# Block-causal attention and a maxout feed-forward in one kernel: group 2's q and k requested behind group 1's, its scores and exps among the units of M, group 3's q and k beside w1

## The chip, the cores and the metric

The kernel runs on one core of one Trainium2 chip. The metric is the device time of one execution in microseconds (us). Before the change it is 260.99 us, the median of four runs (259.36 to 264.78).

## What is computed

Eight batches, eight heads, 576 positions of 64 numbers each; the mask is causal by blocks of 64. The attention output, as 4,608 tokens of 512 numbers, goes through a feed-forward layer with two parallel weights and a maximum between them.

```python
scores = scale * np.matmul(q, k.transpose(0, 1, 3, 2))
mask = block_i >= block_j                      # blocks of 64
scores = np.where(mask, scores, -1000000000.0)
attn = np.exp(scores - np.max(scores, axis=-1, keepdims=True))
attn = attn / (np.sum(attn, axis=-1, keepdims=True) + 1e-09)
x = np.matmul(attn, v)                         # then to (B * S, H * D)
h1 = x @ w1
h2 = x @ w2
out = np.maximum(h1, h2) @ w_out
```

## The kernel before, in words

**Groups and pairs.** Two heads make a pair, two pairs a group: pairs 0 and 1 are group 0, pairs 4 and 5 are group 2. A batch has two groups, so groups 0 and 1 (pairs 0 to 3) are batch 0, and group 2 is the first of batch 1. There are 16 groups.

**What happens to a group.** `load_qk` requests q and k of a group (0.59 MB each) by two DMAs on a queue, SP's as a rule. With `gated=True` GpSimd first writes one element of the buffer, and the DMA waits for that write: so the request goes out when GpSimd's own program has come to this place. `cast` makes bf16 of them (on VectorE and ScalarE for group 0, on VectorE for group 1, on GpSimd from group 2 on). `transposes` turns 18 small blocks of q, or of k, on TensorE into two PSUM tiles, which VectorE and ScalarE copy out to `qT` and `kT`. `pad_keys` (GpSimd) makes the padded keys for the blocks in the corner. The scores of a pair go to PSUM in three tiles (`tile_0` to `tile_2`; for batch 0 in four bursts, `burst_p`, `burst_q1` to `burst_q3`), ScalarE takes the exp of each into `aT`, and GpSimd sets the masked corners to zero. `av(p, ts)` multiplies by V (with a column of ones for the sum) and VectorE divides, into `xp`. `x_out` transposes `xp` on TensorE and copies it into `xT`; later groups do this by a DMA transpose.

**The feed-forward part.** max(h1, h2) is written as max(x(w1 - w2), 0) + x w2. So the kernel needs d = w1 - w2 (four pieces, `diff_w`, VectorE), and M = w2 w_out, so that the second part becomes x M. w2 is transposed in four units (`bT_unit`), M is computed in eight units of eight matmuls (`m_unit`; M0 to M3 use the first half of w_out and are copied out by VectorE, M4 to M7 the second half and ScalarE), then come the units h (`h_unit`: four matmuls of 512 columns, and the maximum with zero on VectorE into `g`) and y (`y_unit`: 12 matmuls).

**How the order is set.** The order on every engine is that of the program: it is written out by hand. `fill(n)` puts the next n parts of the feed-forward units into TensorE's stream (a part of M costs 0.5, of w2's transposes 0.25, of h and y 1), in the order bT, M, h, y; a unit of h or y may only come when its tokens are done. `fill_of(g)` shares out what is ready over the groups to come.

**Queues and buffers.** V, w2, w_out and w1 are requested by GpSimd, on one queue, in the order of its program; V, w2 and w_out are cast to bf16 on the way. Scores have two PSUM tiles, everything else on TensorE (transposes, M, h, y, av, x_out) shares four, in turn: the next user of a tile waits for the copy out of the last one. q and k each have three raw buffers, so that group 2's first request needs no earlier buffer to come free; group 3's take those of group 0.

**The lines concerned** (of the kernel before): `load_qk` 107 to 119, `cast` 121 to 127, `load_v` 129, `load_w1` 147, `diff_w` 154, `h_unit` 191, `m_unit` 217, `transposes` 322 to 341 (matmuls 329, copies 337), `scores` 343, `pad_keys` 354, `exp` 371, `mask` 376, `av` 442, `x_out` 482; the hand-written order is lines 556 to 655. Its parts for batch 0 end at line 614; group 2 and M follow down to line 641, group 3 from 642.

Of the kernel before, what the change touches and what calls it, by code (L numbers as in the profile page):

```python
# [14 lines left out]
def kernel(  # L15
# [28 lines left out]
    RPP = S // NP  # L44
# [9 lines left out]
    NCH = 5  # L54
# [52 lines left out]
    def load_qk(g, queues, gated=False):  # L107
        b, u = divmod(g, GPB)
        for nm, src, queue in (("q", q, queues[0]), ("k", k, queues[1])):
            if queue is None:  # L110
                continue
            raws[nm, g] = t = raw.tile([P, 2, RPP * D], FP32, name=f"{nm}raw")
            if gated:
                nc.gpsimd.memset(t[:, 0, :1], 0.0)
            queue.dma_start(
                out=t[:],
                in_=src[b, 4 * u:4 * u + 4].rearrange(
                    "(s h) (p t) d -> (h p) s (t d)", h=2, t=RPP),
            )

    def cast(nm, g, parts):
        t = raws[nm, g].rearrange("p s (t d) -> p t s d", d=D)
        if (nm, g) not in qk_n:
            qk_n[nm, g] = qkn.tile([P, RPP, 2, D], BF16, name=f"{nm}n")
        n = qk_n[nm, g]
        for copy, j0, j1 in parts:
            copy(out=n[:, j0:j1], in_=t[:, j0:j1])  # L127

    def load_v(b, c):
        rows = min(P, S - c * P)  # L130
        nc.gpsimd.dma_start(  # L131
            out=vv_r[b % NV][P - rows:, c, :, :D],
            in_=v[b, :, c * P:c * P + rows, :].rearrange("h p d -> p h d"),
        )
# [12 lines left out]
    def load_w1(j):  # L147
        w1_raw[j] = wraw.tile([P, NDM, WB], FP32, name="w1raw")
        nc.gpsimd.dma_start(out=w1_raw[j][:], in_=w1r[:, :, j * WB:(j + 1) * WB])
# [4 lines left out]
    def diff_w(j):  # L154
        nc.vector.tensor_sub(d_sb[:, :, j * WB:(j + 1) * WB], w1_raw[j][:], w2_sb[j])
# [9 lines left out]
    SP, ACT = nc.sync, nc.scalar  # L165
# [4 lines left out]
    nc.vector.memset(zeros[:], 0.0)  # L170
    nc.scalar.activation(out=warm[:], in_=warm[:], func=AF.Exp)
    load_qk(1, (SP, SP))
    make_identity(nc, ident)
    for r in range(NV):
        nc.vector.memset(vv_r[r][:, :, :, D:D + 1], 1.0)
# [123 lines left out]
    def fill(n):  # L299
        while n > 0:  # L300
            if not current:
                k = next((k for k, t in enumerate(todo) if t[2] <= done_tokens[0]), None)
                if k is None:
                    return max(0, n)
                current.append(todo.pop(k))
            t = current[0]
            next(t[1])
            n -= t[3]
            t[0] -= 1
            if not t[0]:  # L310
                current.pop()
        return 0
# [10 lines left out]
    def transposes(nm, g, copies):  # L323
        n = qk_n.pop((nm, g))
        pts = [ps_m.tile([P, RPP, NP], BF16, name=f"ps_{nm}T", tag="m") for _ in range(2)]
        for j in range(RPP):
            for i in range(2):
                r = slice(i * NP, (i + 1) * NP)
                nc.tensor.transpose(  # L329
                    pts[i][:, j, :], n[r, j].rearrange("p s d -> p (s d)"), ident[r, r],  # L330
                )

        def copy_out(which=(0, 1), part=(0, NP), copy=None):
            p0, p1 = part
            for i in which:
                t = (qT_r if nm == "q" else kT_r)[(2 * g + i) % NT]
                (copy or copies[i])(  # L337
                    out=t[:, p0 * RPP:p1 * RPP].rearrange("q (p j) -> q p j", j=RPP),
                    in_=pts[i][:, :, p0:p1].rearrange("q j p -> q p j"),
                )  # L340
        return copy_out
# [12 lines left out]
    def pad_keys(p):  # L354
        nc.gpsimd.tensor_copy(
            out=kz_r[p % NT].rearrange("p (a c) -> p a c", c=BLK)[:, 0:3:2],
            in_=kT_r[p % NT][:, S - 3 * BLK:].rearrange("p (a c) -> p a c", c=BLK)[:, 0:3:2],
        )
# [39 lines left out]
    def burst_q3(p, warm=0):  # L398
        burst(p, ((3, 384, 192),), 1408, warm)
# [11 lines left out]
    def tile_0(p):  # L411
        u = ps_s.tile([P, 2, 512], FP32, name="ps_s", tag="s")
        scores(p, u, 0, 0, 0, 512)
        return lambda: (exp(p, u, 512, 0), mask(p, 0))

    def tile_1(p):
        u = ps_s.tile([P, 2, 512], FP32, name="ps_s", tag="s")
        scores(p, u, 0, 0, 512, 64)
        scores(p, u, 64, 1, 128, 448)
        return lambda: (exp(p, u, 512, 512), mask(p, 576))  # L420

    def tile_2(p):
        u = ps_s.tile([P, 2, 512], FP32, name="ps_s", tag="s")
        corner_scores(p, u, 320)
        scores(p, u, 0, 2, 256, 320)
        scores(p, u, 384, 3, 448, P)

        def out():
            exp(p, u, 512, 1024)
            nc.scalar.activation(  # L430
                out=aT_r[p % NA][BLK:, :, 1536:AW], in_=u[BLK:, :, 320:320 + BLK],
                func=AF.Exp, scale=scale,
            )
            mask(p, 1024)
            mask(p, 1344)
        return out

    def region(*tiles):
        for out in tiles:
            out()  # L440

    def av(p, ts):
        b, hp = divmod(p, HP)
        vv = vv_r[b % NV]
        a = aT_r[p % NA]
        n = len(ts)
        h0 = hp // 2 * 4 + hp % 2
        if p % 2 == 0 and ts[0] == 0:
            xps[p // 2] = xpool.tile([P, 2, NCH, 2, D], BF16, name="xp")
        xp = xps[p // 2]  # L450
        po = ps_m.tile([P, n, 2, D + 1], FP32, name="ps_o", tag="m")
        n_mm = 2 * sum(t + 1 for t in ts)
        mm = 0
        for gi, t in enumerate(ts):
            for hh in range(2):
                for c in range(t + 1):
                    a0 = a_col(p, c, t)
                    nc.tensor.matmul(  # L458
                        po[:, gi, hh, :], a[:, hh, a0:a0 + P], vv[:, c, h0 + 2 * hh, :],
                        start=(mm == 0), stop=(mm == n_mm - 1),  # L460
                    )
                    mm += 1
        rec = small.tile([P, 3, 2, 1], FP32, name="rec")
        nc.vector.reciprocal(rec[:, :n, :, 0], po[:, :, :, D])  # L464
        nc.vector.tensor_mul(  # L465
            xp[:, :, ts[0]:ts[0] + n, p % 2].rearrange("q s t d -> q t s d"), po[:, :, :, :D],
            rec[:, :n].to_broadcast([P, n, 2, D]),
        )
# [13 lines left out]
    def x_out(g, t0=0, t1=NCH, copies=(dve, dve)):  # L482
        b, u = divmod(g, GPB)
        if x_by_dma(g):
            if u == GPB - 1:
                done_tokens[0] = (b + 1) * S
            return
        xp = xps[g]
        n = t1 - t0
        n_odd = min(t1, NCH - 1) - t0  # L490
        pe = ps_m.tile([P, 2, n, BLK], BF16, name="ps_xe", tag="m")
        po = ps_m.tile([P, 2, n_odd, BLK], BF16, name="ps_xo", tag="m")
        for s in range(2):
            for t in range(t0, t1):
                src = xp[:, s, t].rearrange("p a d -> p (a d)")
                nc.tensor.transpose(pe[:, s, t - t0, :], src[:BLK], ident[:BLK, :BLK])
                if t < NCH - 1:
                    nc.tensor.transpose(po[:, s, t - t0, :], src[BLK:], ident[BLK:, BLK:])
        dst = xT[:, 2 * u:2 * u + 2, b * S + t0 * P:b * S + t1 * P].rearrange(
            "p s (t h w) -> p s t h w", h=2, w=BLK)  # L500
        copies[0](out=dst[:, :, :, 0], in_=pe[:])
        copies[1](out=dst[:, :, :n_odd, 1], in_=po[:])
        if u == GPB - 1:
            done_tokens[0] = min(b * S + t1 * P, (b + 1) * S)
# [86 lines left out]
    burst_p(3, 1)  # L591
    masks_p(2)
    masks_p(3)
    load_qk(2, (SP, SP), gated=True)
    load_w1(0)
    fill(2)
    av(1, [2, 3, 4])
    burst_q1(2)
# [11 lines left out]
    av(3, [0, 1])  # L610
    burst_q2(3)
    av(2, [2, 3, 4])
    burst_q3(3)
    masks_q(3)
    load_w1(3)
    cast("q", 2, ((pool, 0, RPP),))
    load_qk(3, (SP, SP), gated=True)
    cast("k", 2, ((pool, 0, RPP),))
    load_v(1, 0)
    fill(8)  # L620
    av(3, [2, 3, 4])
    x_out(1, 0, NCH, (act, act))
    fill(4)
    transposes("q", 2, (dve, act))()
    fill(4)
    transposes("k", 2, (dve, act))()
    pad_keys(4)
    pad_keys(5)
    load_v(1, 1)
    diff_w(0)  # L630
    fill(4)
    region(tile_0(4), tile_1(4))
    load_v(1, 2)
    load_v(1, 3)
    fill(8)
    region(tile_2(4), tile_0(5))
    load_v(1, 4)
    diff_w(1)
    fill(8)
    region(tile_1(5), tile_2(5))  # L640
    diff_w(2)
    cast("q", 3, ((pool, 0, RPP),))
    cast("k", 3, ((pool, 0, RPP),))
# [89 lines left out]
```

## Time and profile before

| | |
|---|---|
| runs (us) | 259.36, 262.26, 264.78, 259.72 |
| the profiled execution | 259.36, with a span of 257.5 |
| mean granted TensorE clock | 1.00 |
| moved by DMA | 41.28 MB, mean 160 GB/s |

The span is the time between the first and the last instruction that the profile shows. The page cuts it into 40 equal slices of 6.4 us; each digit is the busy share of a slice in tenths, and the last two rows tell how busy the 16 DMA engines were on the mean, and what they moved in GB/s:

```profile
PE   8897899999999999999999999999999999999995
DVE  4986559656684348433843384338442743543300
ACT  2876394687665857585758574857485611000111
POOL 1984495576556344634472447253721100000000
DMA  7999999989999686998798869985977061202122
GB/s 249 211 160 262 335 306 71 356 99 234 190 159 267 131 270 52 233 155 224 116 265 134 255 73 252 149 244 77 92 130 112 6 89 51 74 6 75 43 106 98
```

PE is TensorE's matmul, DVE VectorE, ACT ScalarE, POOL GpSimd. The stages around the change lie in the first seven slices: up to about 24 us the attention of batch 0, with w2's transposes among it; from 24.91 to about 38 us the units of M with the scores and exps of group 2; then units of h, and group 3's transposes at 42.13 and 44.12 us. From about 47 us on the loop over the groups runs, and after 217 us only h and y are left.

DMA requests of this stage, with the start of the issue in us: group 2's q and k 18.50 and 18.91; group 3's 27.03 and 27.51; the four pieces of w1 18.61, 21.57, about 22.3 and 24.25; the halves of w_out 14.42 and 16.63.

### The profile page before, as it was taken

Reading aid. Unit: us, or ns where it says so; the run is one execution under the profiler, and the core shown is the slowest. Engines: PE = TensorE matmul, PEld = TensorE weight load, DVE = VectorE, ACT = ScalarE, POOL = GpSimd, SP = SyncE. Lnnn points to the kernel's source line nnn. Section 1 sums busy time; section 2 is a strip of 40 time slices with the busy share of each in tenths; the row PEclk is TensorE's granted clock in tenths of the full one; section 3 lists DMA queues with packets and bytes.
Section 4 is the critical chain, followed back from the end, with each engine's and each line's share of the span. In section 5 each row is a group of like instructions: output and inputs, shape, how many; then the busy total and the mean of one; then the engine's idle time right before and its main releaser. Section 6 shows DMA issues by size and latency. Waiting matters only on the chain.

```text
span 257.5 us, 7082 instructions
## 1 busy us (share of the span) xinstructions
PE 248.5 (97%) x2948; PEld 135.6 (53%) x2948; DVE 135.3 (53%) x279; ACT 142.6 (55%) x200; POOL 106.9 (42%) x269
## 2 busy tenths in 40 slices
PE   8897899999999999999999999999999999999995
PEld 2465754556555555555555555555555555444444
DVE  4986559656684348433843384338442743543300
ACT  2876394687665857585758574857485611000111
POOL 1984495576556344634472447253721100000000
PEclk9999999999999999999999999999999999999999
DMA  7999999989999686998798869985977061202122
GB/s 249 211 160 262 335 306 71 356 99 234 190 159 267 131 270 52 233 155 224 116 265 134 255 73 252 149 244 77 92 130 112 6 89 51 74 6 75 43 106 98
DMA packets 71264, 41.28 MB, mean 160 GB/s; under 512 B 53569, under 2 KB 58049, under 8 KB 71233
## 3 DMA queue, kind: packets, MB, share of 16 engines
q1 hardware_dynamic: 28544, 31.27, 43.8%
q0 software_dynamic: 42272, 8.92, 38.8%
q10 hardware_dynamic: 416, 0.66, 0.7%
q8 instruction: 23, 0.38, 0.7%
q14 instruction: 9, 0.07, 0.1%
HBM read 34.60 MB, written 9.44 MB: 171 GB/s over the span
## 4 chain that ended last, share of the span: by engine, by line
PE 83%; POOL 6%; DMA 6%; ACT 1%; issue 1%; DVE 1%; ACTq 0%; POOLq 0%
PE ps_y L240 36%; PE ps_h L198 23%; PE ps_o L458 10%; PE ps_s L348 7%; DMA wo_sb<-in_moe_w_out_dram 4%; POOL vv L131 3%; PE ps_qT L329 2%; DMA qraw<-in_q_dram 2%; PE ps_kT L329 2%; PE ps_M L221 2%; POOL xT L152 1%; PE ps_y L255 1%; POOL aT L377 1%; POOL qn L127 1%; ACT aT L372 1%
## 5 line engine op out<-in xcount | busy, mean ns | idle before, releaser
L372 ACT ACTIVATE aT<-ps_s 128x1024 bf16<-128x1024 f32 (+2 forms) x100 | 95.9, 996 | 22.4 <-PE ps_s L348 20.7
L240 PE MATMUL ps_y<-wo_sb,g 128*128 128x512 bf16 x280 | 70.2, 379 | 0.0
L198 PE MATMUL ps_h<-xT,d_sb 128*128 128x512 bf16 x288 | 68.9, 380 | 0.0
L203 DVE TENSOR_SCALAR g<-ps_h 128x512 bf16<-128x512 f32 x72 | 49.5, 689 | 32.9 <-PE ps_h L198 32.0
L377 POOL MEMSET aT<- 64x128 bf16 x128 | 23.3, 202 | 84.5 <-ACT aT L372 83.7
L458 PEld LDWEIGHTS <-aT 128*128 128x128 bf16 x960 | 37.4, 98 | 14.0 <-issue 0.5
L245 ACT COPY y<-ps_y 128x512 f32<-128x512 f32 x31 | 18.2, 586 | 45.4 <-PE ps_y L240 37.0
L464 DVE RECIPROCAL rec<-ps_o 128x4 f32<-128x4 f32 (+1 forms) x64 | 12.0, 187 | 58.6 <-PE ps_o L458 57.7
L198 PEld LDWEIGHTS <-d_sb 128*128 128x128 bf16 x288 | 26.0, 98 | 30.4 <-issue 3.1
L240 PEld LDWEIGHTS <-g 128*128 128x128 bf16 x280 | 25.7, 98 | 29.3 <-issue 1.9
L458 PE MATMUL ps_o<-vv,aT 128*128 128x65 bf16 x960 | 39.7, 194 | 0.0
L240 PE MATMUL ps_y<-m_sb,xT 128*128 128x512 bf16 x140 | 38.2, 380 | 0.0
L131 POOL DMA_DIRECT2D vv<-in_v_dram x40 | 33.7, 848 | 0.9 <-issue 0.5
L348 PE MATMUL ps_s<-qT,kT 64*128 64x128 bf16 (+6 forms) x344 | 31.6, 280 | 1.4 <-ACT kT L337 0.7
L465 DVE TENSOR_TENSOR xp<-ps_o,rec 128x256 bf16<-128x256 f32 (+1 forms) x64 | 31.4, 491 | 2.2
L240 PEld LDWEIGHTS <-xT 128*128 128x128 bf16 x140 | 12.1, 98 | 15.3 <-issue 3.7
L127 POOL CAST qn<-qraw 128x1152 bf16<-128x1152 f32 (+1 forms) x15 | 17.1, 1137 | 6.6 <-DMA qraw<-in_q_dram 6.5
L337 ACT COPY qT<-ps_qT 128x576 bf16<-128x576 bf16 x15 | 9.6, 639 | 17.9 <-PE ps_qT L329 17.9
L348 PEld LDWEIGHTS <-kT 64*128 64x128 bf16 x344 | 12.0, 94 | 12.2 <-issue 7.9
L337 ACT COPY kT<-ps_kT 128x576 bf16<-128x576 bf16 x15 | 9.6, 638 | 14.1 <-PE ps_kT L329 13.3
L127 POOL CAST kn<-kraw 128x1152 bf16<-128x1152 f32 x14 | 16.1, 1152 | 1.5 <-DMA kraw<-in_k_dram 1.1
L337 DVE COPY qT<-ps_qT 128x576 bf16<-128x576 bf16 x17 | 12.7, 750 | 0.9 <-PE ps_qT L329 0.9
(58 smaller groups left out, 149.9 us busy)
## 6 DMA issues: line engine op xcount, KB each, us to landing
qraw<-in_q_dram SPq DMA_DIRECT2D x16, 576.0 KB, 4.2
out_dram<-y SPq DMA_DIRECT2D x35, 256.0 KB, 3.3
kraw<-in_k_dram SPq DMA_DIRECT2D x15, 576.0 KB, 5.7
vv<-in_v_dram POOLq DMA_DIRECT2D x32, 128.0 KB, 5.1
w1raw<-in_moe_w_dram POOLq DMA_DIRECT2D x4, 512.0 KB, 13.1
xT<-in_moe_w_dram POOLq DMA_DIRECT2D x4, 256.0 KB, 6.2
wo_sb<-in_moe_w_out_dram POOLq DMA_DIRECT2D x2, 512.0 KB, 11.8
kraw<-in_k_dram ACTq DMA_DIRECT2D x1, 576.0 KB, 5.5
```

Of the source, the lines that this page charges most:

```text
L127: copy(out=n[:, j0:j1], in_=t[:, j0:j1])
L131: nc.gpsimd.dma_start(out=vv_r[b % NV][P - rows:, c, :, :D], in_=v[b, :, c * P:c * P + rows, :].rearrange("h p d -> p h d"),)
L198: nc.tensor.matmul(pt[:], d_sb[:, c, f * P:(f + 1) * P], xT[:, c, t0:t0 + SPAN], start=(c == 0), stop=(c == NDM - 1),)
L203: nc.vector.tensor_scalar_max(g[:, f], pt[:], 0.0)
L240: nc.tensor.matmul(py[:], lhs, rhs, start=(n == 0), stop=(n == len(terms) - 1),)
L245: (dve if i < 1 else act)(out=y[:], in_=py[:])
L337: (copy or copies[i])(out=t[:, p0 * RPP:p1 * RPP].rearrange("q (p j) -> q p j", j=RPP), in_=pts[i][:, :, p0:p1].rearrange("q j p -> q p j"),)
L348: nc.tensor.matmul(ps[:, hh, col:col + w], kT[r, k0:k0 + P], qT[r, q0:q0 + w], start=True, stop=True,)
L372: nc.scalar.activation(out=aT_r[p % NA][:, :, a0:a0 + w], in_=ps[:, :, :w], func=AF.Exp, scale=scale,)
L377: (eng or nc.gpsimd).memset(aT_r[p % NA][BLK:, :, a0:a0 + BLK], 0.0)
L458: nc.tensor.matmul(po[:, gi, hh, :], a[:, hh, a0:a0 + P], vv[:, c, h0 + 2 * hh, :], start=(mm == 0), stop=(mm == n_mm - 1),)
L465: nc.vector.tensor_mul(xp[:, :, ts[0]:ts[0] + n, p % 2].rearrange("q s t d -> q t s d"), po[:, :, :, :D], rec[:, :n].to_broadcast([P, n, 2 ...
```

## The change

Four things are moved; no instruction on TensorE is added or removed.

- Group 2's q and k are requested right behind group 1's on SP's queue, without the gate.
- GpSimd casts group 2's q and k right behind the first request of w1, and they are transposed among the last bursts of batch 0 (q before `burst_q3(3)`, k behind it).
- The first unit of M, the second `av` of pair 3 and then the first two score tiles of group 2 follow; the other tiles stand between the units of M. `x_out(1)` comes behind M1 instead of behind the `av`, and VectorE copies it out instead of ScalarE. The requests for V of batch 1 and the weight differences move along; the fills ahead of group 3 put one unit of h less before its cast.
- Group 3's q and k are requested (gated) behind the last request of w1.

```diff
@@ set-up
     load_qk(1, (SP, SP))
+    load_qk(2, (SP, SP))
     make_identity(nc, ident)
...
@@ hand-written order
     masks_p(2)
     masks_p(3)
-    load_qk(2, (SP, SP), gated=True)
     load_w1(0)
+    cast("q", 2, ((pool, 0, RPP),))
+    cast("k", 2, ((pool, 0, RPP),))
     fill(2)
...
     burst_q2(3)
     av(2, [2, 3, 4])
+    transposes("q", 2, (dve, act))()
     burst_q3(3)
     masks_q(3)
     load_w1(3)
-    cast("q", 2, ((pool, 0, RPP),))
     load_qk(3, (SP, SP), gated=True)
-    cast("k", 2, ((pool, 0, RPP),))
-    load_v(1, 0)
-    fill(8)
-    av(3, [2, 3, 4])
-    x_out(1, 0, NCH, (act, act))
-    fill(4)
-    transposes("q", 2, (dve, act))()
-    fill(4)
     transposes("k", 2, (dve, act))()
     pad_keys(4)
     pad_keys(5)
+    fill(4)
+    av(3, [2, 3, 4])
+    region(tile_0(4), tile_1(4))
+    load_v(1, 0)
     load_v(1, 1)
-    diff_w(0)
     fill(4)
-    region(tile_0(4), tile_1(4))
+    x_out(1)
+    fill(8)
+    region(tile_2(4), tile_0(5))
     load_v(1, 2)
     load_v(1, 3)
+    diff_w(0)
     fill(8)
-    region(tile_2(4), tile_0(5))
+    diff_w(1)
+    region(tile_1(5), tile_2(5))
     load_v(1, 4)
-    diff_w(1)
     fill(8)
-    region(tile_1(5), tile_2(5))
     diff_w(2)
     cast("q", 3, ((pool, 0, RPP),))
     cast("k", 3, ((pool, 0, RPP),))
```

## The prediction

> **What bounds the kernel now.** I read first the share of each engine and the waits of TensorE (columns: us in total, times, longest us).
>
> ```profile
> PE 248.5 (97%) x2948; PEld 135.6 (53%) x2948; DVE 135.3 (53%) x279; ACT 142.6 (55%) x200; POOL 106.9 (42%) x269
> ...
> PE ps_M L221 <- DMA wo_sb<-in_moe_w_out_dram: 1.5, 1, 1.5
> PE ps_xe L496 <- DVE xp L465: 0.7, 1, 0.7
> PE ps_qT L329 <- POOL qn L127: 0.5, 1, 0.5
> PE ps_s L348 <- ACT aT L430: 0.4, 1, 0.4
> ```
>
> TensorE works 97% of the span, and from 60 to 200 us its busy time is 139.96 of 140 us. The diff adds and removes no matmul (5,898 rows on TensorE's queue in both programs), so it can only win or lose idle time ahead of 47 us, and the waits above hold nearly all there is to win. Next, the chain of waits (start us, us, what) and the timeline around them:
>
> ```profile
> 14.42 10.45 DMA wo_sb<-in_moe_w_out_dram
> 24.91 1.92 PE ps_M L221 x16
> ...
> 40.34 1.75 POOL qn L127
> 42.13 0.44 PE ps_qT L329 x18
> ```
>
> ```profile
> 38.00 1.22 DVE L155 TENSOR_TENSOR d_sb<-w1raw,xT 128x1024 bf16<-128x1024 f32 x1
> 39.25 0.69 DVE L203 TENSOR_SCALAR g<-ps_h 128x512 bf16<-128x512 f32 x1
> 39.86 1.22 DVE L155 TENSOR_TENSOR d_sb<-w1raw,xT 128x1024 bf16<-128x1024 f32 x1
> 40.99 1.28 DVE L203 TENSOR_SCALAR g<-ps_h 128x512 bf16<-128x512 f32 x2
> 44.59 0.76 DVE L337 COPY kT<-ps_kT 128x576 bf16<-128x576 bf16 x1
> ```
>
> M0, the first unit of M, waits until 24.91 for the first half of w_out; TensorE had come to it at 23.42. Group 3's transposes wait for a cast on GpSimd; VectorE is never long idle there. Last, the transfers: landing times of single issues, and windows (last column GB/s).
>
> ```profile
> vv<-in_v_dram POOLq DMA_DIRECT2D x1, 64.0 KB, 4.6
> wo_sb<-in_moe_w_out_dram POOLq DMA_DIRECT2D x1, 512.0 KB, 10.4
> ...
> 5.00:6.25 1.25, 1.25 (x4) 0.45 (x3) 0.41 (x1) 0.00 (x0) 0.38 (x2) 1.00 1.05 411
> 10.00:11.25 1.25, 1.04 (x8) 0.30 (x6) 1.25 (x2) 1.25 (x3) 1.25 (x2) 1.00 2.17 138
> 23.75:25.00 1.25, 0.09 (x1) 0.09 (x2) 0.30 (x1) 0.20 (x1) 0.95 (x2) 1.00 1.18 314
> ```
>
> q, k alone move at 411 GB/s, V alone at 138, w_out beside group 2's q, k at 314 together.
>
> **The early request.** Group 2's q, k (1.18 MB) now go out on SP behind group 1's, whose last issue ends at 2.24 us, in place of 18.50 and 18.91. SP has nothing else queued until 27 us; two gating memsets (0.1 us each) leave GpSimd. The data then moves beside V and w2 instead of beside w_out. How much the GpSimd queue (V, w2, w_out, w1 in order) loses is not in this trace. Not below nothing, since the added bytes go to the same engines; at most the 1.18 MB at 411 GB/s = 2.9 us. Nearest row: the four w2 pieces land at 16.0, 17.8, 18.9 and 20.6 (issue plus landing time), 1.53 each, so that the first w_out half, twice as large, would take 3.07 after them; it took 24.86 - 20.6 = 4.3 beside group 2's q, k: 1.2 lost. In that stretch those moved (314 - 0.524 MB/4.3 us = 192 GB/s) x 4.3 = 0.83 MB, so 1.45 us per MB, and 1.7 us for 1.18 MB. I take 1.7, as the row with the same two streams.
>
> V's last piece lands at 9.8 + 4.6 = 14.4; the av of pair 0 (24 matmuls from 14.49, 0.75 us in the chain) reaches its last six at 15.05: 0.65 of slack. The w2 pieces have 0.7 to 1.3. So TensorE stands 1.7 - 0.65 = 1.0 us at this av (bounds 0 and 2.2), and the exps queued behind it move with it. w_out: 24.9 + 1.7, less the 1.2 it no longer loses: 25.4 (bounds 23.7 and 26.6).
>
> The Trainium skill ("DMA: Bandwidth & Descriptors", Queues, rings and completion order) has each DMA engine take turns between its queues packet by packet. If I make that an estimate with equal time for each, the queue loses the whole 2.9, and M0 below begins at 26.6 instead of 25.4; it speaks against the change more than my row does.
>
> **Casts and transposes of group 2.** Two casts on GpSimd (1.14 and 1.15) move from 25.82-29.3 to just behind the first w1 issue (ended 19.4, now 20.4 with the stall). The idle 1.63 us ahead of the masks of pair 2 covers most; these come about 0.5 later, about 22.8, and the av that needs them starts at 22.33 + 1.0 = 23.3, behind their 0.4: nothing. Three w1 issues behind them go out about 2 us later, but the queue has w_out to move until 29.7: nothing. The q, k transposes (18 each, 0.37 in the chain) now stand before M0: +0.74. Their two ScalarE copies (0.64 each) surround pair 3's last exp, whose mask is needed only after M0 (0.96): nothing; without that cover, 0.64.
>
> So TensorE comes to M0 at 23.42 + 1.0 + 0.74 = 25.2, w_out at 25.4: M0 at 25.4, 0.5 later than before.
>
> **M, group 2's scores and exps.** From M0 to group 3's q transposes, before: 42.13 - 24.91 = 17.2. After, by rows of the chain: eight M units at 0.96 = 7.7, second av of pair 3 0.75, x_out 0.37, six score tiles 0.54 + 0.57 + 0.47 = 1.6, and 16 h matmuls at 0.216 = 3.5 (19 before: the fills changed by one h unit less, one matmul more): 13.9. x_out's wait of 0.7 goes, because 1.5 us of scores and M1 now stand between the av and it. By this, the transposes could come at 39.3.
>
> **What is late next.** Four PSUM tiles turn in this pool; the q transposes take those of h0 and h1, and g1 stands on VectorE behind the last weight difference. That needs the last w1 piece: issued 24.25, landed 13.8 later, 38.0. It is requested later but stays behind the same bytes, so I keep 38.0. Difference 1.22, g1 0.69: 39.9. The same difference runs beside GpSimd's q cast, which needs group 3's loads (now requested at about 27, as before, because the masks ahead of their gate wait for pair 3's late exp) and took 1.75 instead of 1.14 beside it; so 39.9 stands as the earliest, not 39.3. Then g2, g3 1.28, q copy 0.76, g4, g5 1.28, k copy 0.76: k is there at 44.0, where it was at 44.59 + 0.76 = 45.35. Earlier by 1.35; two h matmuls (28 done instead of 30) are still owed: 0.43. Sum **-0.9 us**. From there on TensorE is full in both, and the tail is the same.
>
> The profiled execution took 259.36 (span 257.5); the median of the four runs is 260.99, with a second at 259.72 and two at 262.26 and 264.78, which nothing in the profile explains. From the two that agree (259.54): 259.54 - 0.9 = **258.6**.
>
> **Rivals.**
>
> *Late weights (slower).* One mechanism: the GpSimd queue loses the full 2.9 us and gets nothing back beside w_out, so the last w1 lands at 40.9. Difference and g1 end at 42.8, k is there at 46.9: +1.55 + 0.43 = +2.0, 261.5. It decides from the point at which k comes after 45.35 - 0.43 = 44.92, that is, a last w1 piece later than 38.9. For it: 138 GB/s beside a DMA share of 2.17 looks like busy engines. Against: w_out's lost 1.2 us belongs to a neighbour that is gone.
>
> *Free engines (faster).* V and w2 lose nothing: TensorE at M0 at 24.2, the last w1 1.2 earlier at 36.8, k at 42.8: -2.55 + 0.43 = -2.1, 257.4. For it: q, k alone make 411 GB/s, V alone a third. Against: 314 together with w_out, where the two alone would make more.
>
> *Nothing gained, moved only.* A new wait inside the M stage: M4 and M5 are copied out by ScalarE, now behind group 2's exps, and two of these (1.02 each) and the short one (0.27) could hold a PSUM tile for up to 2.3 us. The first 0.6 of it fills the gap from 39.3 to 39.9, so 1.5 of it eats the sum: 259.5. For it: three exps now fall into the stage of the M units that ScalarE copies. Against: ScalarE was idle for 4.94 us before 28.89, and the tile of M4 is asked for again only after three more units (2.9 us).
>
> *A colder TensorE.* The first 512-column matmuls follow each other by 0.43 us, later ones by 0.216. The idle 1.49 before M0 left it fast (16 matmuls of 256 columns in 1.92). If a stall at the first av were over 3 us, the matmuls to M0 (about 7 us) would partly run at half speed, up to +3: 262.5. The skill ("TensorE: Matmul & The Clock Gate", Part 1: The HAM clock gate) puts the return to half speed at an idle window of about 3.4 us; my 1.0, or 2.2 at the bound, stays under it.
>
> **How the numbers follow.** Chances: forecast 0.45, late weights 0.22, free engines 0.13, nothing gained 0.13, colder TensorE 0.07. The forecast's own range is 257.6 to 259.8. The range over all, 256.9 to 261.9, takes in free engines and late weights, and leaves out the cold case and the outer part of both. 1% (2.6 us) is about what a measurement tells from no change: faster by more needs free engines and a little over, 0.12; slower by more is the cold case and the upper part of late weights, 0.15; the rest, 0.73.
>
> **What would show it.** Right: a wait at the first av of pair 0 of about 1 us on V's transfer; M0 at 25 to 26 and hardly waiting; no wait at x_out; k copy of group 3 ending near 44. Wrong: M0 after 27, the last w1 after 38.9, a stall between 47 and 60 us beyond the 0.4 of before, or cast times on GpSimd that hold back the av of pair 2.

## The result and the profile after

| | before | after |
|---|---|---|
| median (us) | 261.81 (258.18 to 264.93, 64 runs) | 262.52 (261.07 to 263.74, 43 runs) |
| the profiled execution | 259.36, span 257.5 | 261.17, span 259.3 |
| its mean granted clock | 1.000 | 0.993 |
| the first unit of M begins | 24.91 | 28.1 |
| k of group 3 copied out (end of the copy) | 45.35 | 46.69 |

The ratio is 1.0084, with a 95% interval of 1.0066 to 1.0102: 0.8% slower, where 258.6 us was forecast, 0.9 us below the two runs of before that it started from. The ratio leaves out executions more than 1.5% above the fastest of their kernel, and with before these are executions at a lower clock. The clock is half of the story: in 100 executions of before that ran beside the experiments, 52 had a mean granted clock of at least 0.998, with a median of 259.35 us, and 48 a lower one, with a median of 262.75. Of the executions of after none is above 0.993. So after always takes the time that before takes in its worse half, and at full clock (the third experiment) it is 1.6 us behind before.

The page of after, its engines and the granted clock in 40 slices of 6.5 us:

```profile
PE 250.4 (97%) x2948; PEld 136.6 (53%) x2948; DVE 136.4 (53%) x281; ACT 141.5 (55%) x198; POOL 105.4 (41%) x267
...
PEclk9988999999999999999999999999999999999999
```

TensorE is busy for 1.9 us more with the same 2,948 matmuls; some of them ran slower, and the third and fourth slice (13 to 26 us) say where. The waits of TensorE (us in total, times, longest):

```profile
PE ps_o L459 <- DMA vv<-in_v_dram: 1.4, 3, 1.0
...
PE ps_qT L330 <- DVE g L204: 0.4, 1, 0.4
PE ps_kT L330 <- DVE xp L466: 0.4, 1, 0.4
```

The waits on w_out (1.5) and at `x_out` (0.7) are gone as forecast, and a wait on V has come. The chain of waits (start us, us, what):

```profile
9.78 7.59 DMA vv<-in_v_dram
17.37 0.04 issue
17.41 0.49 PE ps_o L459 x6
...
27.10 0.57 DVE xp L466
27.67 0.05 issue
27.72 0.43 PE ps_kT L330 x17
28.15 0.98 PE ps_M L222 x8
```

The chain now comes from V's last piece, which lands at 17.4; before it was there at 14.4. The `av` of pair 0 ends 2.5 us later (its reciprocal at 17.95 instead of 15.43). Behind that, the windows (PE, PEld, DVE, ACT, POOL busy; granted clock; DMA share; GB/s):

```profile
13.75:15.00 1.25, 1.07 (x15) 0.50 (x13) 1.25 (x3) 0.93 (x1) 1.09 (x2) 1.00 2.42 154
15.00:16.25 1.25, 0.74 (x15) 0.42 (x10) 0.66 (x3) 1.10 (x2) 0.53 (x1) 1.00 2.35 127
16.25:17.50 1.25, 0.52 (x12) 0.42 (x11) 0.00 (x0) 0.01 (x1) 0.20 (x1) 0.95 1.62 172
17.50:18.75 1.25, 1.25 (x13) 0.62 (x13) 0.75 (x2) 0.10 (x1) 0.00 (x0) 0.50 1.47 193
18.75:20.00 1.25, 1.25 (x13) 0.42 (x12) 0.60 (x2) 0.87 (x2) 0.76 (x2) 0.50 1.45 197
20.00:21.25 1.25, 1.25 (x21) 0.95 (x21) 0.03 (x1) 1.08 (x2) 0.66 (x3) 0.68 1.45 195
```

From about 17.4 to 20.8 us TensorE has half its clock, though it had been busy for 2.33 of the 3.75 us ahead (the first three rows), and its longest single wait was 1.0 us. "Busy 1.25 of 1.25" in the rows at 0.50 is therefore not full work. In before the same 3.75 us were full:

```profile
13.75:17.50 3.75, 3.73 (x66) 2.35 (x67) 2.88 (x8) 3.53 (x5) 2.85 (x7) 1.00 1.26 159
```

Why is V late? The transfers by queue from 7.5 to 9 us (packets, MB, share of 16 engines' time; q0 is GpSimd's queue, q1 SP's), in before and then in after:

```profile
q0 software_dynamic: 692, 0.09, 92.1%
q1 hardware_dynamic: 156, 0.32, 58.5%
```

```profile
q1 hardware_dynamic: 274, 0.59, 106.2%
```

GpSimd issues its first request for V at 6.2 us in both. In before its first packet moves at 8.0, in after at 10.5; until then only SP's queue, with q and k of groups 1 and 2, moves. The delay shrinks along GpSimd's queue: the first V piece lands 2.9 us later than before (13.2), the last w2 piece 2.3 (22.9), the first half of w_out 0.7 (25.5), and the last w1 piece 3.7 us *earlier* (34.3).

Last, VectorE ahead of group 3 (start us, us, line; in brackets the idle time before):

```profile
39.69 0.69 DVE L204 TENSOR_SCALAR g<-ps_h 128x512 bf16<-128x512 f32 x1 [2.19 <-PE ps_h L199]
40.30 1.85 DVE L155 TENSOR_TENSOR d_sb<-w1raw,xT 128x1024 bf16<-128x1024 f32 x1
42.08 1.87 DVE L204 TENSOR_SCALAR g<-ps_h 128x512 bf16<-128x512 f32 x3
```

The last weight difference is ready to go from 34.3 on, but stands in the program behind g0, which waits for TensorE's h0. VectorE is idle for 2.19 us ahead of it.

### The profile page after: what moved, and what is told of

Same layout as the page of the kernel before. It is cut to its first block, busy times and chain, and to the rows that moved or that the text cites. A ratio compares the mean times of both kernels' runs of the same rounds, so it can differ in the third digit from the quotient of the medians.

```text
span 259.3 us, 7080 instructions
## 1 busy us (share of the span) xinstructions
PE 250.4 (97%) x2948; PEld 136.6 (53%) x2948; DVE 136.4 (53%) x281; ACT 141.5 (55%) x198; POOL 105.4 (41%) x267
## 4 chain that ended last, share of the span: by engine, by line
PE 86%; DMA 5%; ACT 3%; DVE 2%; POOL 2%; issue 1%; ACTq 0%
PE ps_y L241 35%; PE ps_h L199 23%; PE ps_o L459 11%; PE ps_s L349 8%; DMA vv<-in_v_dram 3%; ACT aT L373 2%; PE ps_M L222 2%; DMA qraw<-in_q_dram 2%; PE ps_kT L330 2%; PE ps_qT L330 2%; POOL vv L131 1%; PE ps_y L256 1%; DVE g L204 1%; PE ps_s L367 1%; DVE d_sb L155 1%
## 5 line engine op out<-in xcount | busy, mean ns | idle before, releaser
L459 PE MATMUL ps_o<-vv,aT 128*128 128x65 bf16 x960 | 40.7, 194 | 1.4 <-DMA vv<-in_v_dram 1.4
L127 POOL CAST qn<-qraw 128x1152 bf16<-128x1152 f32 (+1 forms) x15 | 16.5, 1097 | 4.6 <-DMA qraw<-in_q_dram 4.5
L338 ACT COPY kT<-ps_kT 128x576 bf16<-128x576 bf16 x15 | 9.6, 639 | 14.4 <-PE ps_kT L330 14.4
L127 POOL CAST kn<-kraw 128x1152 bf16<-128x1152 f32 x14 | 17.1, 1223 | 0.2 <-DMA kraw<-in_k_dram 0.2
```

The source lines that it names most:

```text
L338: (copy or copies[i])(out=t[:, p0 * RPP:p1 * RPP].rearrange("q (p j) -> q p j", j=RPP), in_=pts[i][:, :, p0:p1].rearrange("q j p -> q p j"),)
L459: nc.tensor.matmul(po[:, gi, hh, :], a[:, hh, a0:a0 + P], vv[:, c, h0 + 2 * hh, :], start=(mm == 0), stop=(mm == n_mm - 1),)
```

## The experiments

"Beside" means runs of before on the same chip. Medians are over 10 to 12 executions, unless said otherwise.

**1. Which part costs: the early request or the new order?** The first kernel is before with the early request alone; the second is after with group 2's q and k requested on the gate behind `load_w2(2)`, at about 13.4 us; the third is after with seven warm-up matmuls in the wait on V; the fourth moves the last weight difference ahead of g0.

```diff
# e1_early_only, from before
     load_qk(1, (SP, SP))
+    load_qk(2, (SP, SP))
...
-    load_qk(2, (SP, SP), gated=True)
     load_w1(0)
# e2_late_request, from after
-    load_qk(2, (SP, SP))
...
     load_w2(2)
+    load_qk(2, (SP, SP), gated=True)
# e3_warm, from after
     burst_q2(1, 1)
+    warm_up(7)
     av(0, [2, 3, 4])
# e4_diff3_early, from after
     diff_w(2)
+    diff_w(3)
     cast("q", 3, ((pool, 0, RPP),))
     cast("k", 3, ((pool, 0, RPP),))
     fill(4)
-    diff_w(3)
```

> The kernel before with one edit: group 2's q, k requested behind group 1's; the order of all else as before. Theory 1 (V held back, then half clock): V's last piece lands near 17.4 us as in the changed kernel (14.4 before), TensorE idles about 2.5 us ahead of the end of pair 0's av, the granted clock falls to about 0.5 for one window, and M0 starts at 26.8 to 27.5; time 1.0 to 2.5 us above before (ratio 1.004 to 1.010). Theory 2 (the loss comes from the new order behind M0: the last weight difference behind g0, GpSimd's casts): the order is that of before, so the time is within 0.5 us of before (ratio 0.998 to 1.002).

262.91, ratio 1.0105 [1.0067, 1.0143]; six executions at 0.993, six at 0.987. The request alone costs all that the change costs: the waits on V are 2.1 us here, and the fall of the clock is there in each execution.

> The changed kernel with group 2's q, k requested (gated) behind the third w2 request, about 13.4 us, in place of behind group 1's; all else as changed. Theory 1: V's last piece lands at 14.4 as before, no wait at pair 0's av, clock 1.0 throughout, M0 at 25 to 26 instead of 28.1; time 1.5 to 3 us below the changed kernel, at or below before (ratio 0.992 to 1.000). Theory 2: M0 is earlier, but group 3's scores stay later than before's 45.46, ratio 1.004 to 1.008.

262.55, ratio 1.0089 [1.0054, 1.0123]. I had expected this to be no slower than before, and missed. V is in time again (last piece at 14.7), but the delay has only changed its victim. TensorE's waits:

```profile
PE ps_bT L210 <- DMA xT<-in_moe_w_dram: 3.4, 2, 1.8
```

The last w2 piece lands at 24.3 instead of 20.6, the transposes of w2 wait 3.4 us for it, and the clock falls again (0.70 from 21.25 to 25 us, 0.50 from 25 to 28.75).

> The changed kernel with seven warm-up matmuls of 512 columns (1.5 us at full clock) ahead of pair 0's second av, to keep TensorE busy while it waits for V. V lands at 17.4 as in the changed kernel. If the half clock is a cost of its own (theory 1): granted clock 1.0 from 16 to 22 us, M0 1.0 to 1.6 us earlier than 28.1, time 0.7 to 1.6 below the changed kernel (ratio to before 1.002 to 1.006). If the clock matters nothing, because other waits (DMA of w2, w_out) end last: M0 within 0.3 of 28.1 and ratio 1.007 to 1.010.

260.9, ratio 1.0028 [0.999, 1.0067]; 11 of 12 executions at 0.998 or more. V landed no sooner than in after (18.3 in the profiled execution), and the clock stayed. The two windows of this kernel that answer to the rows of after:

```profile
13.75:17.50 3.75, 2.96 (x35) 1.64 (x35) 1.41 (x4) 1.77 (x2) 1.79 (x4) 1.00 2.13 148
17.50:21.25 3.75, 2.90 (x51) 1.92 (x51) 1.62 (x5) 2.00 (x3) 1.44 (x5) 1.00 1.45 196
```

From the end of pair 0's `av` to the first unit of M it takes 9.0 us instead of 10.1. So the fall costs 1.1 us in the profiled executions and 262.52 - 260.9 = 1.6 us in the medians, where 20 of the 44 executions of after are at 0.987, with a median of 263.0 (22 are at 0.993, with 261.9). The kept traces at 0.987 (the second, fourth, eleventh and twelfth kernels) show one fall of 6.8 us where after has one of 3.4; in the fourth it lasts from 16.2 to 23.0.

> The changed kernel with the last weight difference placed right behind the third, so that VectorE does it in its idle 2.19 us ahead of g0 instead of behind g0. Theory 1: V, clock and M0 as in the changed kernel (28.1); only the waits of 0.43 and 0.18 at group 3's transposes go, time 0.4 to 0.9 below the changed kernel (ratio 1.004 to 1.007). Theory 2: the whole loss goes, group 3's scores start at 45 to 45.5, ratio 1.000 or below.

261.69, ratio 1.0053 [1.0015, 1.0091], with the clock as low as in after. From the first unit of M to group 3's scores it takes 17.82 us instead of 18.66: the place of one instruction on VectorE's queue is worth 0.8.

**2. The two repairs together, each on the other base, and the opposite request.** The fifth kernel fills the wait on w_out in before with warm-up matmuls; the sixth joins the third and fourth; the seventh asks for group 2's q and k later than before does, at 21.9 us; the eighth is the first with warm-up matmuls.

```diff
# e5_before_warm, from before
     load_v(1, 0)
+    warm_up(6)
     fill(8)
# e6_warm_diff3, from after: the edits of e3_warm and e4_diff3_early
# e7_later_request, from before
-    load_qk(2, (SP, SP), gated=True)
     load_w1(0)
...
     masks_q(2)
+    load_qk(2, (SP, SP), gated=True)
     load_w1(1)
# e8_early_warm, from e1_early_only
     burst_q2(1, 1)
+    warm_up(7)
     av(0, [2, 3, 4])
```

> The kernel before with six warm-up matmuls (1.3 us) ahead of M0, where TensorE is idle for 1.49 us. Of 35 runs of before beside the first experiments, 16 had a mean granted clock of 0.998 or 1.0 (median 259.3) and 19 had 0.993 or less (262.4 and more). If it is this idle stretch that lets the clock fall in some executions: all runs at 0.998 or 1.0, median 259.0 to 259.8, some 2 us below the median of before. If the fall has another place (the start at 7.5 to 11 us, or 13 to 20): the same mixture as before, median 261 to 262, and never faster than 259.

260.08, ratio 0.9995 [0.9948, 1.0042], beside 261.35 for before with all its executions. 11 of 12 at 0.998 or more, where 14 of 29 of before were. So before loses its clock at the idle time ahead of the first unit of M. That the place is this one rests on these counts (and those of the ninth and tenth kernels below), since the trace of before is of an execution that kept its clock.

> The changed kernel with both repairs: seven warm-ups ahead of pair 0's second av, and the last weight difference behind the third. If the two costs add: the warm-ups' 1.5 us and the 0.8 us of the difference, median 260.0 to 260.5 at clock 1.0, still 0.7 to 1.2 above before's runs at clock 1.0 (259.3), because V is still 2.9 us late. If they cover each other: 260.7 to 261.2.

260.03, ratio 1.0006 [0.9975, 1.0038], all 12 at 0.998 or more. The two edits add up, and bring the ratio back to 1; against before at full clock (259.35 beside it) 0.7 us are still lost.

> The first experiment (before's order, group 2's q, k requested early) with the seven warm-ups ahead of pair 0's second av, so that the clock holds. Beside e3 (the changed order, early request, clock held: 260.9) it prices the order alone, beside before at clock 1.0 (259.3) the early request alone. If the request costs its stall of 2.7 us less what the earlier landings give back: 261.2 to 262.2, so the new order is worth 0.3 to 1.3 us. If the new order is the loss: 259.3 to 260.3, below e3.

260.8, ratio 1.0026 [0.9994, 1.0057], all 12 at 0.998 or more. It lies between my two ranges, 261.2 to 262.2 and, if the new order were the loss, 259.3 to 260.3. Against the first kernel the fall is worth 2.1 us. With the third kernel (1.0028) this puts the new order as a whole at nothing (0.0002), and with the sixth (1.0006) at a gain of about 0.002 without the late difference, both within intervals of some 0.003 to either side.

> The kernel before with group 2's q, k requested 3 us later (behind the masks of pair 2, about 21.5 us instead of 18.5), nothing else moved. If the GpSimd queue loses time to whatever q, k bytes are beside it: the first half of w_out lands at 23.4 to 24.0 instead of 24.86 and M0 starts at 23.4 to 24.0; q, k land about 29 and 31.5, so that group 2's transposes wait for their casts 0.5 to 1.5 us; time 259.3 to 261 in runs at clock 1.0. If w_out is slow by itself: M0 stays at 24.9.

267.29, ratio 1.0278 [1.0216, 1.0339] (4 executions); I expected 259.3 to 261 and missed. The first half of w_out, now alone, landed only 0.4 earlier (24.5); but it lands at 24.3, 25.4 and 26.4 in the tenth, fifth and ninth kernels, which request it as before does, so one trace doesn't price this. The waits of TensorE:

```profile
PE ps_kT L329 <- POOL kn L127: 2.4, 1, 2.4
PE ps_qT L329 <- POOL kraw L114: 2.3, 1, 2.3
...
PE ps_M L221 <- DMA wo_sb<-in_moe_w_out_dram: 0.9, 1, 0.9
```

GpSimd stood 5.4 and 3.7 us for q and k, and all that it does behind the casts came late. TensorE also has half its clock from 30.9 to 41.1 us in this execution, so a part of the loss is the clock's. The moved request has no better place on this side either; how much of w_out's transfer time had been lost to group 2's q and k stays open.

**3. A version that beats both?** If the idle time ahead of the first unit of M costs before half of its executions 3 us, then `av(3, [2, 3, 4])`, which needs nothing of w_out, should come ahead of it. The ninth kernel does this with three warm-up matmuls, the tenth without.

```diff
# e10_av_first, from before (e9_av_first_warm: warm_up(3) ahead of av)
     load_v(1, 0)
-    fill(8)
     av(3, [2, 3, 4])
+    fill(8)
```

> The kernel before, without the early request, with the second av of pair 3 ahead of M0 and M1 instead of behind them, and three warm-ups ahead of it: TensorE does the av while it waits for w_out, and x_out finds its input ready. If the idle stretch at 23.4 us is both a loss of 1.5 us and what lets the clock fall: M0 at 24.9 to 25.2, no wait of 0.7 at x_out, 12 of 12 runs at clock 0.998 or more, median 257.8 to 258.6, below before and the changed kernel. If w_out moves later with it, or the next wait (group 3's cast) takes it all: 259.2 or more.

259.18, ratio 0.9959 [0.9927, 0.9992], beside 259.71; all 12 at 0.998 or more. Against before at full clock (259.30 beside it) only 0.1 us is gained, where I had expected about 1 unless w_out came later. It did in the profiled execution: it landed at 26.4, TensorE waited 1.9 us for it in one piece, and the clock was 1.00 all the same. Beside it, the stretch ahead of the fall in the fourth kernel, which was fuller:

```profile
22.75:26.50 3.75, 1.90 (x36) 1.27 (x32) 1.66 (x5) 0.93 (x2) 1.67 (x5) 1.00 1.16 312
```

```profile
12.45:16.20 3.75, 2.50 (x28) 1.16 (x29) 2.71 (x6) 2.34 (x4) 2.89 (x6) 1.00 2.49 142
```

So the busy share alone does not tell whether the clock falls: 51% kept it, 67% lost it.

> The same without the three warm-ups. The av fills 0.75 of the 1.49 idle us. If that is enough for the clock: as e9, 257.8 to 258.6, nearly all runs at 0.998 or more. If the clock needs the stretch fuller: a part of the runs at 0.993 and 1.5 to 3 us longer, as in before.

258.5, ratio 0.9967 [0.9931, 1.0003]; 11 of 12 at 0.999 or more. The window of 21.25 to 25 us, in before and in this kernel:

```profile
21.25:25.00 3.75, 2.26 (x50) 1.82 (x48) 2.50 (x6) 2.55 (x4) 2.85 (x6) 1.00 1.25 284
```

```profile
21.25:25.00 3.75, 3.46 (x76) 2.78 (x73) 2.57 (x7) 2.60 (x4) 2.80 (x7) 1.00 1.26 278
```

TensorE is busy for 1.2 us more in this window, most of it the `av`: there is no wait on w_out and none at `x_out`, and group 3's scores begin at 43.70 instead of 45.46. At full clock that is 258.5 against 259.3; against the executions of before at a lower clock (7 of the 23 beside it, median 262.04) it is 3.5 us. The interval of the tenth ends just above 1, that of the ninth just below.

**4. Why did GpSimd's queue move nothing?** Either its small rows lose against the larger ones of q and k, or what is asked for later begins later. The eleventh kernel (one execution) puts a w2 piece, whose packets are four times V's, first on the queue; the twelfth asks for V 4.5 us earlier, ahead of group 2's q and k.

```diff
# e11_w2_first, from after
+    load_w2(0)
     for c in range(NCH):
         load_v(0, c)
-    load_w2(0)
# e12_v_early, from after
-    cast("q", 0, ((dve, 0, 7), (pool, 7, RPP)))
-    cast("k", 0, ((act, 0, 5), (dve, 5, RPP)))
     for c in range(NCH):
         load_v(0, c)
+    cast("q", 0, ((dve, 0, 7), (pool, 7, RPP)))
+    cast("k", 0, ((act, 0, 5), (dve, 5, RPP)))
```

> The changed kernel with the first w2 piece (rows of 1 KB) requested by GpSimd ahead of the five V pieces (rows of 256 bytes), so that a large-row transfer stands first on GpSimd's queue while SP's four requests for groups 1 and 2 are still moving. If V got nothing because of its small rows: GpSimd's queue moves packets from 8 us on, at about the rate it has beside q, k later (near half the time), and w2's piece lands at 11 to 12 us. If GpSimd's queue gets nothing because SP's requests were all queued before it: no packet of it until about 11.5 us, w2's piece lands at 12.5 to 13.5, and V after it, its last piece at 18 to 19.

263.9 in one execution. The w2 piece is issued at 6.3, moves its first packet at 10.6 and lands at 13.5. With its larger rows it starts no sooner than V did: the size of the rows does not decide when the queue starts.

> The changed kernel with the V requests ahead of GpSimd's own cast, so that they go out at 2 to 6 us instead of 6.2 to 10.5, when SP's requests are being issued too. If the order of requests decides, V shares the engines from 4 us on, its last piece lands at 10 to 13, the waits at pair 0's av go and the clock holds; group 0's q, k come up to 3 us later, so the time is 259 to 262. If SP's queue goes first whatever the order: V lands after 11.9 us as before, last piece 16 to 17.4, time as the changed kernel, 261 to 263.

263.09, ratio 1.0074 [1.003, 1.0117]. V is issued from 1.67 us on, moves its first packet at 6.3, and lands from 13.6 to 18.9, no sooner than in after. From 9 to 10.5 us in this kernel:

```profile
q1 hardware_dynamic: 220, 0.48, 92.6%
q0 software_dynamic: 219, 0.03, 28.3%
```

Once it has started, it gets packet for packet with SP's queue, but its packets are of 128 bytes and the others of some 2,200.

The four starts (1.9 us after the issue in before, 4.4 and 4.3 in after and the eleventh kernel, 4.6 in the twelfth) fit one reading: the first packet waits until most of what stood on SP's queue at its issue has moved (by sums over half-microsecond windows, 0.73 of 0.86 MB in before and 1.72 of 2.08 MB in after). It was not tried by itself, and stays a reading.

## Why the prediction was wrong, by its steps

**The size of the queue's loss.** The step that failed first is the 1.7 us that GpSimd's queue would lose. V lost 2.9 to 3.0, the upper bound. I took the price from one row of w_out beside q and k, by assuming that w_out's transfer starts when the last w2 piece has landed. That time is no firm price: it is 4.3 us in before, and 3.9 to 5.5 in the fifth, ninth and tenth kernels, which request w_out as before does; without q and k it is 3.6 in the seventh kernel and 2.6 in after, where I had 3.1. (The third w2 piece landed at 19.2, not 18.9; nothing rests on it.) The rows that were there would have given the size. q and k alone move 274 packets in 1.5 us on 16 engines, 88 ns per packet and engine; V alone 1,836 packets in 1.5 us (after, 12 to 13.5), 13 ns. Side by side (twelfth kernel) a pair takes 1.5 x 16 / 219 = 110 ns, which is no less than 88 + 13. So the engines' time adds up here, and by this reading the transfer that ends last loses all of the other's 1.18 MB, in whatever order they move.

The Trainium skill ("DMA: Bandwidth & Descriptors", Queues, rings and completion order) lets an engine take turns packet by packet. The 219 to 220 packets of the twelfth kernel agree; that V's queue moves none for 4.4 us after its first issue, while the other moves 274 in 1.5 us of it, is not what it describes. The 2.9 us that I had worked out by it, and set aside for my row, is what came.

**The stall at pair 0's `av`** was thus 2.5 us instead of 1.0: right in place and in mechanism, mis-sized with the step above.

**The colder TensorE** had a chance of 0.07 and the condition "a stall over 3 us". That is the second failed step, worth 1.6 us in the medians: the longest wait was 1.0 us in the profiled execution, and the clock fell in all. That the stretch behind the wait on V is the place is shown by the warm-ups, which held the clock in the third, sixth and eighth kernels. What in such a stretch decides is not shown: 62% busy over 3.75 us here and 67% in the fourth kernel came ahead of a fall, 60% in the profiled execution of before (21.25 to 25 us) and 51% in that of the ninth did not. Before falls in about half of its executions; the runs at 262.26 and 264.78, which I said that nothing in the profile explains, lie among its executions at a lower clock (261.34 to 266.46). The Trainium skill ("TensorE: Matmul & The Clock Gate", Part 1: The HAM clock gate) gives a window of about 3.4 us. The time at half speed agrees, 17.4 to 20.8 us. That an idle window of that length is needed for the fall does not agree with the 1.0 us here; that 1.9 us in one piece passed in the ninth kernel does.

**From 23.42 to the first unit of M.** Forecast: 1.0 of stall and 0.74 of transposes, with w_out at 25.4 as the bound. w_out landed at 25.5, as forecast, and bounded nothing; that its number came out is luck, since the 1.7 in it and the 1.2 taken off it were both wrong (2.3 lost by the last w2 piece, 1.6 of it won back behind that). Measured: 23.42 + 2.5 + 0.74 = 26.7; 0.4 for a PSUM tile that k's transposes wait for (the tile of the `av` that VectorE still divides into `xp`), which I had not seen; and the rest to 28.1, 1.0, is the half clock.

**From there on the forecast's length held.** From the first unit of M to group 3's q transposes: 14.1, forecast 13.9. `x_out`'s wait went, and ScalarE's exps between the units of M cost nothing that shows, so the rival "nothing gained" did not come. To the end of k's copy it is 18.6 us, forecast 18.6, which is in part luck, since the cause is another: I had VectorE bound by the last w1 piece at 38.0. It landed at 34.3, and what held the difference was its place behind g0; the fourth kernel took that away and 0.8 us with it. The difference beside GpSimd's cast took 1.85, where I had 1.22 from before; there the cast took 1.75 and the difference kept its 1.22, in after the second cast took 2.14 as well.

**The sum.** The end of k's copy is 46.69 - 44.0 = 2.7 later than forecast, and the first unit of M 28.1 - 25.4 = 2.7: in the sum, all that is wrong lies ahead of M. With the two matmuls owed, -0.9 + 2.7 = +1.8 us, which is the difference of the spans (259.3 - 257.5).

**The rival "late weights"** gave 261.5, near the time measured, for a wrong reason: the queue did lose 2.9 us, but w1 came earlier, not at 40.9. I let the loss run down the whole queue, while it shrank along it (2.9 at V, 2.3 at w2, 0.7 at w_out); whose data was due first (V's, with 0.65 us of slack) decided.

## What to carry to other kernels

A request moved forward does not use idle transfer time unless the engines are idle there: add up the engine time of both queues, and charge all of it to the transfer that is due first. A TensorE with short waits that add up (here to 1.4 of 3.75 us) can lose half its clock for 3.4 or 6.8 us; how much idle time it bears these runs do not settle. So a median between two clusters of times, or a mean granted clock that differs between executions, is a reason to look for such a stretch and to fill it with work that does not depend on what is awaited. And on an engine that takes its program in order, an instruction whose data is there is still late if it stands behind one that waits.

## What was unexpected of the hardware

Three things. The clock of TensorE fell with no single wait over 1.0 us, seven added matmuls in the gap held it (11 of 12 executions), and in another kernel it stayed through a wait of 1.9 us. A GpSimd queue moved nothing for 4.4 us after its first issue while SP's moved 0.39 MB per us, and (asked for earlier) took turns packet for packet (219 to 220). And one kernel had two clusters of times, with medians of 259.35 and 262.75 us, that meet at 261.1 to 261.3 and that the clock of each execution tells apart.
